# A wave of attention chunks beside an expert layer: three kinds of TensorE work put into one place of the timetable

## The chip, the cores and the metric

The kernel runs on one core of a Trainium2 chip, as one launch. The metric is device time in microseconds: the median of three runs, 939.94 us (939.4 to 940.61). Five engines work side by side and wait for each other through semaphores: TensorE (PE; its weight loads have a row of their own, PEld), VectorE (DVE), ScalarE (ACT), GpSimd (POOL) and SyncE (SP, which issues most DMAs).

## The reference

Three layers follow each other: a linear attention with a decaying state, a bilinear feed-forward layer, and a mixture of eight experts of which each token takes two.

```python
for t in range(S):                     # attention, B=4, H=8, S=768, D=48
    cur = einsum('bhd,bhe->bhde', u[None] * kt, vt)
    y[:, :, t] = einsum('bhd,bhde->bhe', rt, state + cur)
    state = wt[..., None] * state + einsum('bhd,bhe->bhde', kt, vt)
h = (x @ w1) * (x @ w2) @ w3           # x: 3072 x 384, w1, w2: 384 x 1024
x = h @ w_out
logits = x @ w_gate + log1p(exp(x @ w_noise)) * noise   # then the best 2 of 8 experts
out[mask] += weight * (relu(x[mask] @ w1[e]) @ w2[e])
```

## The kernel before

The 3072 tokens are cut into 24 chunks of 128 (j = 0 to 23), six to a batch. A chunk's attention has these parts, each a function of j:

- `pre_scan`, `pre_rec`, `pre_k`, `pre_r` (mostly DVE, `pre_rec` step 0 on ACT) turn decays, keys and queries into scaled keys `kt` and queries `rt`; `pre_u`, `pre_c`, `pre_d` (POOL, DVE, ACT) make the diagonal term, and `pre_d` fills the tile `am` with it.
- `at_A` (A, line 240): key-query products, 8 matmuls on halves of 64 rows of the array (`tile_position` is the row 0 or 64). The trace shows each as two, so 16. `at_ov` then copies them under a mask into `am` (DVE, L245).
- `at_T` (T, L250): 4 transposes of the keys on the full array, copied by ACT into `kn`.
- `at_kv` (kv, L261): state products, 8 matmuls (16 in the trace) on halves of 64 columns of the array; DVE adds and scales them (`sc`, `stmp`, `snew`, L265 to L272), and ACT copies the state into `S`.
- `at_y` (y, L300): outputs, on quarters of 32 columns; 56 matmuls in the trace (32 where a batch begins, since there is no state yet). ACT and DVE split the result into `xh` and `xl`. The last chunk of a batch has no T and no kv.

The feed-forward layer goes in 12 groups of two chunks. A group has 12 places: `mo_ab` eight times (18 matmuls of 256 columns on the full array each: x @ w1 into one bank, x @ w2 into another; ACT copies the first to `ac`, DVE multiplies to `pp`, ACT and `low_p` on DVE split that into `ph` and `pl`) and `mo_x` four times (12 matmuls of 400 columns). All of them are on the full 128x128 array, and they are the filling between the attention parts.

A timetable sets what stands beside what. `at(slot, fn, ...)` puts a call into a list, and `run_todo(slot)` runs the list at the end of the place with that number: slots below 0 lie in the weight folding that comes first (0 to about 65 us), slot 12g+i is place i of group g. So two parts of one slot stand next to each other on every engine, in the order in which they were put in. Before, the attention of chunk j from 4 on begins at slot 6j-12 and takes one slot for each of A, `at_ov`, T, kv and y (`start` and `att_steps`), the preparations lie up to 7 slots earlier (`PRE`), and tables (`ATT`, `PREL`) give the first chunks. DVE runs in written order; the order on the other engines comes from a list scheduler that follows it closely. After the last group (about 450 us) eight experts follow, which the change doesn't touch.

Of the kernel before, what the change touches and what calls it, by code (L numbers as in the profile page):

```python
# [22 lines left out]
NCH = N // P  # L23
CPB = S // P
# [47 lines left out]
def tile_kernel(ctx: ExitStack, tc: tile.TileContext, dt, nat, w3t, wout, w1, w2, e1, e2, cf, ci, out):  # L72
# [17 lines left out]
    def c(n):  # L90
        o, w = CF[n]
        return cft[:, o:o + w]
# [84 lines left out]
    def load_dt(j):  # L177
        DT[j] = att.tile([P, NDT], F32, name="dtc")
        sp.dma_start(out=DT[j], in_=dt[j])

    def load_na(j):
        NA[j] = att.tile([P, NNAT], F32, name="natc")
        sp.dma_start(out=NA[j], in_=nat[j])
# [4 lines left out]
    def pre_scan(j):  # L188
        FG[j] = att.tile([P, 8 * (HC + 1)], F32, name="fg")
        dve.tensor_tensor_scan(out=FG[j], data0=DT[j][:, 8 * P:], data1=d1, initial=0.0,  # L190
                               op0=OP.mult, op1=OP.add)

    def pre_rec(j, step):

        fa = fgv(j)[:, :, 1:]
        if step == 0:
            RC[j] = att.tile([P, 8, HC], F32, name="rc", bufs=1)
            KT[j] = att.tile([P, 4, 2, HC], F32, name="kt")
            act.activation(out=RC[j], in_=fa, func=AF.Ln)
            act.activation(out=RC[j], in_=RC[j], func=AF.Exp, scale=-1.0)  # L200
        else:
            t = KT[j].rearrange("p a s i -> p (a s) i")
            dve.tensor_tensor(out=t, in0=fa, in1=RC[j], op=OP.mult)
            dve.scalar_tensor_tensor(RC[j], t, -2.0, RC[j], op0=OP.add, op1=OP.mult)

    def pre_k(j):
        k = DT[j][:, 4 * P:8 * P].rearrange("p (a s i) -> p a s i", s=2, i=HC)
        dve.tensor_tensor(out=KT[j][:, :, 0], in0=k[:, :, 0], in1=fgv(j)[:, 1::2, :HC], op=OP.mult)
        dve.scalar_tensor_tensor(KT[j][:, :, 1], k[:, :, 1], -1.0, RC[j][:, 0::2], op0=OP.mult, op1=OP.mult)

    def pre_r(j):
        RT[j] = att.tile([P, 4, 2, HC], F32, name="rt")
        r = DT[j][:, :4 * P].rearrange("p (a s i) -> p a s i", s=2, i=HC)
        dve.scalar_tensor_tensor(RT[j][:, :, 0], r[:, :, 0], -1.0, RC[j][:, 1::2], op0=OP.mult, op1=OP.mult)
        dve.tensor_tensor(out=RT[j][:, :, 1], in0=r[:, :, 1], in1=fgv(j)[:, 0::2, :HC], op=OP.mult)

    def pre_u(j):
        t = att.tile([P, DM], F32, name="rku", bufs=1)
        on = dve if 2 <= j < 5 else pool
        on.tensor_tensor(out=t, in0=NA[j][:, :DM], in1=NA[j][:, DM:2 * DM], op=OP.mult)  # L220
        on.tensor_tensor(out=t, in0=t, in1=c("u"), op=OP.mult)
        KS["u", j] = t
# [12 lines left out]
    def at_A(j):  # L235

        for a in range(4):
            for hb in range(2):
                q = slice(HC * hb, HC * hb + D)
                pe.matmul(bST[hb][:, P * a:P * a + P], KT[j][q, a].rearrange("p s i -> p (s i)"),  # L240
                          RT[j][q, a].rearrange("p s i -> p (s i)"), start=True, stop=True,
                          tile_position=(HC * hb, 0))

    def at_ov(j, hb):
        dve.copy_predicated(out=AM[j][:, hb::2], mask=ic("mask")[:, None, :].to_broadcast([P, 4, P]),  # L245
                            data=bST[hb].rearrange("p (h t) -> p h t", h=4))

    def at_T(j):
        for a in range(4):
            pe.transpose(bY[:, P * a:P * a + P], KT[j][:, a].rearrange("p s i -> p (s i)"), ident)  # L250
        KN[j] = att.tile([P, 4, P], F32, name="kn", bufs=1)
        act.copy(out=KN[j].rearrange("p a t -> p (a t)"), in_=bY)
# [4 lines left out]
    def at_kv(j):  # L257
        kv = bK[:, :4 * D].rearrange("p (a e) -> p a e", a=4)
        for a in range(4):
            for hb in range(2):  # L260
                pe.matmul(kv[64 * hb:64 * hb + 64, a], KN[j][:, a, 64 * hb:64 * hb + 64],  # L261
                          vv(j, 2 * a + hb)[:, 16 * hb:16 * hb + D], start=True, stop=True,
                          tile_position=(0, 64 * hb))
        sc = att.tile([P, 4], F32, name="sc")
        dve.tensor_tensor(out=sc, in0=fgv(j)[:, 0::2, HC], in1=fgv(j + 1)[:, 1::2, HC], op=OP.mult)  # L265

        new = att.tile([P, 4, D], F32, name="snew", bufs=2)
        src = kv
        if j % CPB:
            src = att.tile([P, 4, D], F32, name="stmp", bufs=1)  # L270
            dve.tensor_tensor(out=src, in0=kv, in1=KS["s", j], op=OP.add)
        dve.tensor_tensor(out=new, in0=src, in1=sc[:, :, None].to_broadcast([P, 4, D]), op=OP.mult)  # L272
        KS["s", j + 1] = new
        for hb in range(2):
            q = slice(64 * hb, 64 * hb + D)
            act.copy(out=St[(j + 1) % 2][q, :, D * hb:D * hb + D], in_=new[q])

    def at_y(j):
        first = j % CPB == 0
        yv = bY[:, :3 * P].rearrange("p (k t) -> p k t", k=3)  # L280
        qs = []
        for q in range(4):
            lst = []
            for kb in range(3):
                a, b = PIECES[kb][q]
                if b is None:
                    hs, so = ((a, 32 * (a % 2)),), 64 * (a % 2)
                else:
                    hs, so = ((a, 32), (b, 0)), 32
                ms = [(vv(j, h)[:, o:o + 32], AM[j][:, h, :]) for h, o in hs]  # L290
                if not first:
                    ms.append((St[j % 2][:, a // 2, so:so + 32], RT[j][:, a // 2].rearrange("p s i -> p (s i)")))
                for i, (lt, rh) in enumerate(ms):
                    lst.append((yv[32 * q:32 * q + 32, kb], lt, rh, i == 0, i == len(ms) - 1, (0, 32 * q)))
            qs.append(lst)
        for i in range(max(map(len, qs))):
            for q in range(4):
                if i < len(qs[q]):
                    o, lt, rh, st, en, tp = qs[q][i]
                    pe.matmul(o, lt, rh, start=st, stop=en, tile_position=tp)  # L300
        g, s = divmod(j, 2)
        if s == 0:
            XH[g] = xp.tile([P, 3, 2 * P], F32R, name="xh")
            XL[g] = xp.tile([P, 3, 2 * P], F32R, name="xl")
        h, l = XH[g][:, :, s * P:s * P + P], XL[g][:, :, s * P:s * P + P]
        act.copy(out=h, in_=yv)
        dve.tensor_tensor(out=l, in0=yv, in1=f(h), op=OP.subtract)

    def att_steps(j):
        last = j % CPB == CPB - 1  # L310

        def s0():
            at_A(j)

        def s1():
            at_ov(j, 0)
            at_ov(j, 1)

        def s2():
            if not last:  # L320
                at_T(j)

        def s3():
            if not last:
                at_kv(j)

        def s4():
            at_y(j)
            if j + 2 < NCH:
                load_na(j + 2)  # L330

        return [s0, s1, s2, s3, s4]

    def pre_steps(j):
        def p2():
            pre_k(j)
            pre_r(j)
            if j + 2 < NCH:
                load_dt(j + 2)

        return [lambda: pre_scan(j), lambda: pre_rec(j, 0), lambda: pre_rec(j, 1), p2, lambda: pre_u(j),
                lambda: pre_c(j), lambda: pre_d(j)]


    woh, wol = [w.rearrange("p (j d) -> p j d", d=XW) for w in (WBh, WBl)]
# [56 lines left out]
    def at(slot, fn, *a):  # L402
        todo.setdefault(slot, []).append((fn, a))
# [2 lines left out]
        for fn, a in todo.pop(k, []):  # L406
            fn(*a)

    def start(j):
        return 6 * (j - 2)  # L410

    PRE = (-7, -7, -4, -3, -2, -2, -1)
    PREL = {0: (-21, -20, -18, -17, -19, -16, -14), 1: (-15, -14, -13, -12, -14, -12, -11),
            2: (-10, -9, 1, 1, -4, 2, 2), 3: (1, 1, 4, 5, 3, 5, 6)}
    ATT = {0: (-14, -13, -14, -13, -12), 1: (-10, -9, -10, -9, -8), 2: (4, 5, 5, 6, 7), 3: (8, 9, 9, 10, 11)}
    WLD = {(0, 0): -16, (0, 1): -14, (1, 0): -8, (1, 1): -6, (0, 2): -4, (1, 2): -2, (0, 3): 1, (1, 3): 3}
    WCV = {(0, 0): -9, (0, 1): -7, (1, 0): -5, (1, 1): -2, (0, 2): 0, (1, 2): 2, (0, 3): 4, (1, 3): 7}
    WSP = (-5, -5, 2, 3)
# [11 lines left out]
            at(slot, cv_w, *k, i)  # L430
    for k, slot in WLD.items():
        at(slot, load_w, *k)
    for j in range(NCH):
        for i, fn in enumerate(att_steps(j)):
            at(ATT[j][i] if j < 4 else start(j) + i, fn)
    for j in range(NCH):
        lo = ATT[j - 2][4] if 2 <= j < 6 else start(j - 2) + 4
        for i, fn in enumerate(pre_steps(j)):
            at(PREL[j][i] if j < 4 else max(lo, start(j) + PRE[i]), fn)
    for slot in WCV.values():  # L440
        if slot >= -5:
            at(slot + 1, flush, 1)
# [590 lines left out]
```

## Time and profile before

| | us |
|---|---|
| median of three runs | 939.94 |
| the profiled execution | 938.21 |
| its span | 936.4 |
| PE busy | 910.5 (97%) |
| PEld busy | 841.4 (90%) |
| DVE busy | 447.3 (48%) |
| ACT busy | 421.9 (45%) |
| POOL busy | 330.3 (35%) |

The profiled execution's span runs from the first instruction to the last; 1.8 us lie around it. A busy PE is not PE at its peak, since the ends of matmuls are modelled and matmuls overlap. What tells how fast PE gets on is the distance from the start of one matmul to the start of the next. In a timeline each row has the start, the time from the first start to the last end of what is merged in the row, the engine, the line, output and input, the shape of the array that is used, the shape of the data and the count.

### The profile page before, as it was taken

How to read it: one execution, taken by the hardware profiler on the slowest of the kernel's cores; microseconds unless marked ns; L12 is line 12 of the kernel's file. 1: busy time of each engine (PE TensorE's matmuls, PEld its weight loads, DVE VectorE, ACT ScalarE, POOL GpSimd, SP SyncE). 2: the span in 40 equal slices, each digit the busy share in tenths (PEclk: the TensorE clock that was granted, in tenths of full speed). 3: DMA queues.
4: the chain of work that ended last, by engine and by line, in shares of the span. 5: the costliest groups of instructions: out<-in, count | busy, mean ns of one | idle time of the engine just before them, and what ended most of it. 6: DMA issues, size and time to landing. Idle time of an engine off the chain costs nothing.

```text
span 936.4 us, 17811 instructions
## 1 busy us (share of the span) xinstructions
PE 910.5 (97%) x7235; PEld 841.4 (90%) x7235; DVE 447.3 (48%) x1126; ACT 421.9 (45%) x875; POOL 330.3 (35%) x267
## 2 busy tenths in 40 slices
PE   8998899999999999999999999999999999999994
PEld 6787799999999999999989989899998989989894
DVE  5889676656665756657364452331313123131320
ACT  7776546446446445454352343433323343332420
POOL 1100110232222131130506626655556565555422
PEclk9999999999999999999999999999999999999997
DMA  9945876445232242220231645344172533614112
GB/s 357 385 157 176 196 139 212 152 139 185 80 117 89 80 125 81 94 77 19 77 128 37 143 135 162 60 133 101 32 172 65 158 64 89 145 28 105 18 20 36
DMA packets 49179, 111.64 MB, mean 119 GB/s; under 512 B 17600, under 2 KB 32192, under 8 KB 49088
## 3 DMA queue, kind: packets, MB, share of 16 engines
q1 hardware_dynamic: 33472, 85.98, 28.6%
q0 software_dynamic: 12160, 19.72, 12.0%
q10 hardware_dynamic: 3456, 4.72, 1.4%
q8 instruction: 58, 0.95, 0.4%
q14 instruction: 33, 0.27, 0.1%
HBM read 88.12 MB, written 22.27 MB: 118 GB/s over the span
## 4 chain that ended last, share of the span: by engine, by line
PE 90%; DVE 4%; ACT 2%; DMA 1%; issue 1%; POOL 0%; POOLq 0%; SPq 0%; ACTq 0%; DVEq 0%
PE pb L170 27%; PE pb L171 26%; PE pb L172 26%; PE pb L300 3%; PE pb L240 2%; PE pb L740 2%; PE pb L778 1%; PE pb L261 1%; PE pb L250 1%; DVE cvz L154 1%; ACT top L145 1%; PE pb L371 0%; DMA raw<-w 0%; ACT w3h L156 0%; DMA rawf<-wout 0%
## 5 line engine op out<-in xcount | busy, mean ns | idle before, releaser
L170 PE MATMUL pb<-XTh,WAh 128*128 128x512 f32 (+1 forms) x384 | 133.3, 348 | 0.0
L171 PE MATMUL pb<-XTl,WAh 128*128 128x512 f32 (+1 forms) x384 | 131.8, 343 | 0.0
L170 PE MATMUL pb<-WBh,HH 128*128 128x384 f32 x384 | 130.9, 341 | 0.0
L172 PE MATMUL pb<-XTh,WAl 128*128 128x512 f32 (+1 forms) x384 | 130.9, 343 | 0.0
L171 PE MATMUL pb<-WBl,HH 128*128 128x384 f32 x384 | 129.6, 337 | 0.0
L172 PE MATMUL pb<-WBh,HH 128*128 128x384 f32 x384 | 129.5, 337 | 0.0
L756 DVE SCALAR_TENSOR_TENSOR HH<-pb,HH 128x256 fp32r<-128x256 f32 (+1 forms) x128 | 71.3, 558 | 116.0 <-ACT HH L755 116.0
L783 POOL DMA_INDIRECT out<-ye,ti x56 | 87.2, 1557 | 107.5 <-ACT ye L773 94.3
L755 ACT ACTIVATE HH<-pb 128x256 fp32r<-128x256 f32 (+1 forms) x128 | 62.8, 491 | 125.0 <-PE pb L172 123.9
L643 POOL DMA_INDIRECT slots<-g_sc,g_si x48 | 52.2, 1088 | 137.0 <-DVE g_si L642 90.8
L220 POOL TENSOR_TENSOR rku<-natc 128x384 f32<-128x384 f32 x21 | 22.1, 1052 | 212.0 <-DMA natc<-nat 139.4
L773 ACT ACTIVATE ye<-pb,ti 128x384 f32<-128x384 f32 x48 | 27.9, 582 | 145.5 <-PE pb L172 129.7
L124 DVE TENSOR_TENSOR XTl<-pb,XTh 128x512 fp32r<-128x512 f32 (+1 forms) x48 | 25.2, 569 | 130.4 <-ACT XTh L123 130.4
L170 PE MATMUL pb<-xh,WBh 128*128 128x256 f32 x288 | 84.0, 291 | 1.7 <-ACT WAh L156 1.4
L170 PE MATMUL pb<-xh,WAh 128*128 128x256 f32 x288 | 82.7, 287 | 1.6 <-DVE W1l L124 1.2
L172 PE MATMUL pb<-xh,WBl 128*128 128x256 f32 x288 | 81.4, 283 | 1.3 <-DVE WBl L161 1.3
L171 PE MATMUL pb<-xl,WBh 128*128 128x256 f32 x288 | 82.2, 285 | 0.0
L172 PE MATMUL pb<-xh,WAl 128*128 128x256 f32 x288 | 81.2, 282 | 0.4 <-DVE WAl L161 0.4
L171 PE MATMUL pb<-xl,WAh 128*128 128x256 f32 x288 | 81.1, 282 | 0.0
L170 PEld LDWEIGHTS pb<-XTh,WAh 128*128 128x128 f32 x384 | 72.2, 188 | 9.6 <-DVE HH L756 1.5
L171 PEld LDWEIGHTS pb<-XTl,WAh 128*128 128x128 f32 x384 | 72.2, 188 | 8.0
L172 PEld LDWEIGHTS pb<-XTh,WAl 128*128 128x128 f32 x384 | 71.8, 188 | 8.2
(174 smaller groups left out, 2185.4 us busy)
## 6 DMA issues: line engine op xcount, KB each, us to landing
dtc<-dt SPq DMA_DIRECT2D x24, 772.0 KB, 4.4
natc<-nat SPq DMA_DIRECT2D x24, 640.0 KB, 5.9
raw<-e SPq DMA_DIRECT2D x18, 768.0 KB, 6.8
raww<-e SPq DMA_DIRECT2D x14, 768.0 KB, 4.4
rawf<-w3t SPq DMA_DIRECT2D x16, 512.0 KB, 7.7
raw<-w SPq DMA_DIRECT2D x8, 768.0 KB, 5.3
x_rows<-xo ACTq DMA_DIRECT2D x24, 192.0 KB, 1.9
out<-zeros SPq DMA_DIRECT2D x4, 1152.0 KB
```

Source lines behind the costliest of these rows:

```text
L124: (on or dve).tensor_tensor(out=l, in0=src, in1=f(h), op=OP.subtract)
L170: pe.matmul(o, wh, xh, start=start, stop=False)
L171: pe.matmul(o, wh, xl, start=False, stop=False)
L172: pe.matmul(o, wl, xh, start=False, stop=stop)
L220: on.tensor_tensor(out=t, in0=NA[j][:, :DM], in1=NA[j][:, DM:2 * DM], op=OP.mult)
L240: pe.matmul(bST[hb][:, P * a:P * a + P], KT[j][q, a].rearrange("p s i -> p (s i)"), RT[j][q, a].rearrange("p s i -> p (s i)"), start=True, ...
L300: pe.matmul(o, lt, rh, start=st, stop=en, tile_position=tp)
L643: ins = pool.indirect_dma_start(out=table, out_offset=bass.IndirectOffsetOnAxis(ap=si[:, i, k:k + 1], axis=0), in_=SC[:, i, k, :], in_offs ...
L755: act.activation(out=Hh[hf][:, ff], in_=bank[:, :n], func=AF.Relu)
L756: dve.scalar_tensor_tensor(Hl[hf][:, ff], bank[:, :n], 0.0, f(Hh[hf][:, ff]), op0=OP.max, op1=OP.subtract)
L773: act.activation(out=y[:n], in_=bank[:n], func=AF.Copy, scale=wt)
L783: ins = pool.indirect_dma_start(out=out, out_offset=bass.IndirectOffsetOnAxis(ap=ti(e, j)[:, 0:1], axis=0), in_=y[:n], in_offset=None, com ...
```

## The change

The slots of the attention parts are moved, and nothing else. For chunk j from 6 on: kv and y of chunk j and A of chunk j+1 share slot 6j-8 (in this order), `at_ov` of j+1 is in the slot behind, and T of chunk j is in slot 6j-11, three before its kv. The scan stands in slot 6j-20, `pre_rec` step 0 in 6j-19, step 1 in 6j-18, `pre_k` in 6j-17, `pre_r` and `pre_c` in 6j-16, `pre_u` in 6j-17, `pre_d` in 6j-15. A table `WHEN` has chunks 0 to 5. Within a slot the order is now that of `STEPS`. No instruction is added or taken away.

```diff
--- before.py
+++ after.py
@@ -306,40 +306,30 @@
         act.copy(out=h, in_=yv)
         dve.tensor_tensor(out=l, in0=yv, in1=f(h), op=OP.subtract)
 
-    def att_steps(j):
-        last = j % CPB == CPB - 1
-
-        def s0():
-            at_A(j)
-
-        def s1():
-            at_ov(j, 0)
-            at_ov(j, 1)
-
-        def s2():
-            if not last:
-                at_T(j)
-
-        def s3():
-            if not last:
-                at_kv(j)
-
-        def s4():
-            at_y(j)
-            if j + 2 < NCH:
-                load_na(j + 2)
-
-        return [s0, s1, s2, s3, s4]
-
-    def pre_steps(j):
-        def p2():
-            pre_k(j)
-            pre_r(j)
-            if j + 2 < NCH:
-                load_dt(j + 2)
-
-        return [lambda: pre_scan(j), lambda: pre_rec(j, 0), lambda: pre_rec(j, 1), p2, lambda: pre_u(j),
-                lambda: pre_c(j), lambda: pre_d(j)]
+    def do_y(j):
+        at_y(j)
+        if j + 2 < NCH:
+            load_na(j + 2)
+
+    def do_kv(j):
+        if j % CPB < CPB - 1:
+            at_kv(j)
+
+    def do_T(j):
+        if j % CPB < CPB - 1:
+            at_T(j)
+
+    def do_ov(j):
+        at_ov(j, 0)
+        at_ov(j, 1)
+
+    def do_r(j):
+        pre_r(j)
+        if j + 2 < NCH:
+            load_dt(j + 2)
+
+    STEPS = (do_kv, do_y, at_A, do_ov, do_T, pre_scan, lambda j: pre_rec(j, 1), pre_k, do_r, lambda j: pre_rec(j, 0),
+             pre_u, pre_c, pre_d)
 
 
     woh, wol = [w.rearrange("p (j d) -> p j d", d=XW) for w in (WBh, WBl)]
@@ -406,13 +396,13 @@
         for fn, a in todo.pop(k, []):
             fn(*a)
 
-    def start(j):
-        return 6 * (j - 2)
-
-    PRE = (-7, -7, -4, -3, -2, -2, -1)
-    PREL = {0: (-21, -20, -18, -17, -19, -16, -14), 1: (-15, -14, -13, -12, -14, -12, -11),
-            2: (-10, -9, 1, 1, -4, 2, 2), 3: (1, 1, 4, 5, 3, 5, 6)}
-    ATT = {0: (-14, -13, -14, -13, -12), 1: (-10, -9, -10, -9, -8), 2: (4, 5, 5, 6, 7), 3: (8, 9, 9, 10, 11)}
+    WHEN = {0: (-13, -12, -14, -13, -14, -21, -18, -17, -17, -20, -19, -16, -14),
+            1: (-9, -8, -10, -9, -10, -15, -13, -12, -12, -14, -14, -12, -11),
+            2: (6, 7, 4, 5, 5, -10, 1, 1, 1, -9, -4, 2, 2),
+            3: (11, 11, 8, 9, 9, 1, 4, 5, 5, 1, 3, 5, 6),
+            4: (16, 16, 11, 12, 13, 7, 8, 9, 9, 7, 10, 10, 11),
+            5: (22, 22, 16, 17, 19, 11, 13, 14, 14, 12, 13, 14, 15)}
+    LATE = (6, 6, 0, 1, 3, -6, -4, -3, -2, -5, -3, -2, -1)
     WLD = {(0, 0): -16, (0, 1): -14, (1, 0): -8, (1, 1): -6, (0, 2): -4, (1, 2): -2, (0, 3): 1, (1, 3): 3}
     WCV = {(0, 0): -9, (0, 1): -7, (1, 0): -5, (1, 1): -2, (0, 2): 0, (1, 2): 2, (0, 3): 4, (1, 3): 7}
     WSP = (-5, -5, 2, 3)
@@ -430,13 +420,9 @@
             at(slot, cv_w, *k, i)
     for k, slot in WLD.items():
         at(slot, load_w, *k)
-    for j in range(NCH):
-        for i, fn in enumerate(att_steps(j)):
-            at(ATT[j][i] if j < 4 else start(j) + i, fn)
-    for j in range(NCH):
-        lo = ATT[j - 2][4] if 2 <= j < 6 else start(j - 2) + 4
-        for i, fn in enumerate(pre_steps(j)):
-            at(PREL[j][i] if j < 4 else max(lo, start(j) + PRE[i]), fn)
+    for i, fn in enumerate(STEPS):
+        for j in range(NCH):
+            at(WHEN[j][i] if j in WHEN else 6 * j - 14 + LATE[i], fn, j)
     for slot in WCV.values():
         if slot >= -5:
             at(slot + 1, flush, 1)
```

PE, chunk 10 and the key-query products of chunk 11, before: kv (L261) stands alone between full-array matmuls; 17 of these come before y (L300), and 30 more before A (L240).

```order
L170 MATMUL pb_67<-xh,WBh 128x256
L261 MATMUL pb_73<-natc,kn 64x48 x8
L171 MATMUL pb_67<-xl,WBh 128x256
...
L172 MATMUL pb_67<-xh,WBl 128x256
L300 MATMUL pb_70<-am,natc 32x128 x4
...
L300 MATMUL pb_70<-rt,S_102 32x128 x4
L170 MATMUL pb_68<-W0h,ph 128x400
...
L172 MATMUL pb_66<-xh,WAl 128x256
L240 MATMUL pb_71<-rt,kt 128x128
...
L240 MATMUL pb_72<-rt,kt 128x128
L170 MATMUL pb_67<-xh,WBh 128x256
```

The same in the changed kernel:

```order
L172 MATMUL pb_67<-xh,WBl 128x256
L261 MATMUL pb_73<-natc,kn 64x48 x8
L300 MATMUL pb_70<-am,natc 32x128 x4
...
L300 MATMUL pb_70<-rt,S_102 32x128 x4
L240 MATMUL pb_71<-rt,kt 128x128
...
L240 MATMUL pb_72<-rt,kt 128x128
L170 MATMUL pb_68<-W0h,ph 128x400
```

kv, y and A now follow each other with no full-array matmul between them. Counted over the program, kv and y of a chunk touch in 16 chunks (4, 6 to 10, 12 to 16, 18 to 22), and y of a chunk touches A of the next in 19 (these, and 5, 11 and 17, which have no kv). Chunk 3 keeps them apart, and its kv is cut in two, with 8 full-array matmuls between.

DVE in slot 1, before: `kt` and `rt` of chunk 2 (L203 to L215), then the scan of chunk 3 (`fg`, L190).

```order
L512 TENSOR_TENSOR pp<-ac,pb_67 128x512
L203 TENSOR_TENSOR kt<-fg,rc 128x512
L204 SCALAR_TENSOR_TENSOR rc<-kt,rc 128x512
L208 TENSOR_TENSOR kt<-dtc,fg 128x4x64
L209 SCALAR_TENSOR_TENSOR kt<-dtc,rc 128x4x64
L214 SCALAR_TENSOR_TENSOR rt<-dtc,rc 128x4x64
L215 TENSOR_TENSOR rt<-dtc,fg 128x4x64
L190 SCALAR_TENSOR_TENSOR fg<-dtc,d_80 128x520
```

In the changed kernel (its L498 is L512 of before):

```order
L498 TENSOR_TENSOR pp<-ac,pb_67 128x512
L190 SCALAR_TENSOR_TENSOR fg<-dtc,d_80 128x520
L203 TENSOR_TENSOR kt<-fg,rc 128x512
L204 SCALAR_TENSOR_TENSOR rc<-kt,rc 128x512
L208 TENSOR_TENSOR kt<-dtc,fg 128x4x64
L209 SCALAR_TENSOR_TENSOR kt<-dtc,rc 128x4x64
L214 SCALAR_TENSOR_TENSOR rt<-dtc,rc 128x4x64
L215 TENSOR_TENSOR rt<-dtc,fg 128x4x64
```

The scan of chunk 3 now stands ahead of the keys and queries of chunk 2, which A of chunk 2 waits for.

DVE in slots 10 and 11, before: the state of chunk 3 (`sc`, `stmp`, `snew`), then the diagonal of chunk 4 (`rku`, `cc`), then `pl`.

```order
L512 TENSOR_TENSOR pp<-ac,pb_67 128x512
L265 TENSOR_TENSOR sc<-fg 128x4
L271 TENSOR_TENSOR stmp<-pb_73,snew 128x192
L272 TENSOR_TENSOR snew<-stmp,sc 128x192
L220 TENSOR_TENSOR rku<-natc 128x384
L221 TENSOR_TENSOR rku<-rku,cft 128x384
L227 TENSOR_REDUCE cc<-rku 128x8
L522 TENSOR_TENSOR pl<-pp,ph 128x512
```

In the changed kernel (L498 is L512 of before, L508 is L522):

```order
L498 TENSOR_TENSOR pp<-ac,pb_67 128x512
L220 TENSOR_TENSOR rku<-natc 128x384
L221 TENSOR_TENSOR rku<-rku,cft 128x384
L227 TENSOR_REDUCE cc<-rku 128x8
L508 TENSOR_TENSOR pl<-pp,ph 128x512
L265 TENSOR_TENSOR sc<-fg 128x4
L271 TENSOR_TENSOR stmp<-pb_73,snew 128x192
L272 TENSOR_TENSOR snew<-stmp,sc 128x192
```

The state's three instructions now stand behind `pl`, which `mo_x` waits for.

## Rows read from the trace of the kernel before

**Rows 1.** The page: busy time of each engine, share of the span, instructions.

```profile
PE 910.5 (97%) x7235; PEld 841.4 (90%) x7235; DVE 447.3 (48%) x1126; ACT 421.9 (45%) x875; POOL 330.3 (35%) x267
```

**Rows 2.** The page: the chain that ended last, by engine.

```profile
PE 90%; DVE 4%; ACT 2%; DMA 1%; issue 1%; POOL 0%; POOLq 0%; SPq 0%; ACTq 0%; DVEq 0%
```

**Rows 3.** Busy us of each engine (instructions) in two stretches, PE clock, DMA.

```profile
100.00:120.00 20.00, 17.25 (x181) 15.50 (x182) 14.07 (x29) 9.61 (x23) 2.78 (x2) 1.00 0.97 135
120.00:140.00 20.00, 20.00 (x230) 19.06 (x232) 13.37 (x25) 7.58 (x18) 2.35 (x2) 1.00 0.64 157
```

**Rows 4.** Timeline of PE around kv of chunk 10.

```profile
222.38 0.28 PE L172 MATMUL pb<-xh,WAl 128*128 128x256 f32 x1
222.50 0.28 PE L170 MATMUL pb<-xh,WBh 128*128 128x256 f32 x1
222.71 0.67 PE L261 MATMUL pb<-natc,kn 128*64 128x48 f32 x16
223.31 0.39 PE L171 MATMUL pb<-xl,WBh 128*128 128x256 f32 x1
223.54 0.28 PE L172 MATMUL pb<-xh,WBl 128*128 128x256 f32 x1
```

**Rows 5.** Timeline of PE around y of chunk 10.

```profile
225.34 0.28 PE L172 MATMUL pb<-xh,WBl 128*128 128x256 f32 x1
225.54 0.43 PE L300 MATMUL pb<-am,natc 128*32 128x128 f32 x8
...
226.88 0.40 PE L300 MATMUL pb<-rt,S 128*32 128x128 f32 x8
227.21 0.45 PE L170 MATMUL pb<-W0h,ph 128*128 128x400 f32 x1
227.50 0.34 PE L171 MATMUL pb<-W0l,ph 128*128 128x400 f32 x1
227.68 0.34 PE L172 MATMUL pb<-W0h,pl 128*128 128x400 f32 x1
```

**Rows 6.** Timeline of PE around A of chunk 11.

```profile
231.52 0.28 PE L172 MATMUL pb<-xh,WAl 128*128 128x256 f32 x1
231.73 1.16 PE L240 MATMUL pb<-rt,kt 48*128 48x128 f32 x16
232.82 0.38 PE L170 MATMUL pb<-xh,WBh 128*128 128x256 f32 x1
233.04 0.28 PE L171 MATMUL pb<-xl,WBh 128*128 128x256 f32 x1
```

**Rows 7.** PE, groups by line, 120 to 430 us: count | busy us, mean ns | idle.

```profile
L300 PE MATMUL pb<-rt,S 128*32 128x128 f32 x360 | 21.8, 273 | 0.0
L240 PE MATMUL pb<-rt,kt 48*128 48x128 f32 x288 | 20.9, 285 | 0.0
L261 PE MATMUL pb<-natc,kn 128*64 128x48 f32 x256 | 10.8, 226 | 0.0
```

**Rows 8.** Timeline of DVE, scan of chunk 3, and state of chunk 3.

```profile
79.09 1.24 DVE L190 TENSOR_TENSOR_SCAN fg<-dtc,d 128x520 f32<-128x520 f32 x1
...
108.82 0.16 DVE L265 TENSOR_TENSOR sc<-fg 128x4 f32<-128x4 f32 x1
...
109.56 0.55 DVE L220 TENSOR_TENSOR rku<-natc 128x384 f32<-128x384 f32 x1
```

**Rows 9.** Timeline of PE, A of chunk 2, and a wait for `pl`.

```profile
79.40 1.16 PE L240 MATMUL pb<-rt,kt 48*128 48x128 f32 x16
...
111.95 0.45 PE L172 MATMUL pb<-W1h,pl 128*128 128x400 f32 x1 [1.33 <-DVE pl L522]
```

**Rows 10.** Timeline of ACT after kv and y of chunk 10.

```profile
224.22 0.71 ACT L276 COPY S<-snew 48x192 f32<-48x192 f32 x2 [0.93 <-DVE snew L272]
...
227.35 0.48 ACT L306 CAST xh<-pb 128x384 fp32r<-128x384 f32 x1 [0.28 <-PE pb L300]
```

**Rows 11.** Timeline of DVE after y of chunk 10.

```profile
227.86 0.56 DVE L307 TENSOR_TENSOR xl<-pb,xh 128x384 fp32r<-128x384 f32 x1 [1.45 <-ACT xh L306]
```

## The prediction

> **What bounds the kernel now.** The page's first part comes first: PE is busy 97% of the span, DVE and ACT under half [rows 1]. The reader is to see that a gain has to come out of PE's own time. The chain of waits agrees: 90% of it is PE [rows 2]. Then the stretches of 20 us, since an average hides stages: from 120 us on PE is busy 20.00 of 20.00 us, at a granted clock of 1.00 (2.4 GHz), in each of the 15 stretches up to 420 us, while between 100 and 120 us it has 17.25 [rows 3]. So in the groups from 1 on no other engine ever ends a wait of PE; there only the distance from one matmul's start to the next one's counts. Before that, PE waits now and then, and a move can cost or give there. After 450 us the program is the same.
>
> The last view is PE's timeline around one chunk, read by starts. Among full-array matmuls a 256-column one starts 0.12 us after the one before (222.38 to 222.50) [rows 4], after a 400-column one it is 0.18 us (227.50 to 227.68) [rows 5]. Where the shape of the array changes, the distance is longer, in three places of each visit:
> - Going in. Before kv 222.50 to 222.71 is 0.21 us, 0.09 over the usual 0.12 [rows 4]; before y 0.20, so 0.08 over [rows 5]; before A 0.21, so 0.09 over [rows 6].
> - Coming out. A merged row ends with its last matmul's end, so the last start is the row's start plus its length less one matmul (226, 273 and 285 ns) [rows 7]. kv: 222.71 + 0.67 - 0.23 = 223.15; eight pairs make seven steps, 0.44 / 7 = 0.06 each; the full matmul starts at 223.31, 0.16 later, 0.10 over a step [rows 4]. y: 226.88 + 0.40 - 0.27 = 227.01; 14 rounds of four make 13 steps from 225.54, 0.11 each; the next one comes 0.20 later, 0.09 over [rows 5]. A: 231.73 + 1.16 - 0.29 = 232.60, steps of 0.125, then 0.22, so 0.09 over [rows 6].
> - The first full matmul after a visit, whose weights could not be loaded ahead. It holds the next one up to 0.23 us instead of 0.12 behind kv [rows 4], 0.29 instead of 0.18 behind y [rows 5], 0.22 instead of 0.12 behind A [rows 6]: 0.11, 0.11 and 0.10 over.
>
> So a visit pays about 0.09 going in and 0.09 + 0.11 coming out, whatever its shape.
>
> **The change, part by part.** Nothing is computed less: the order of PE before and after has the same matmuls.
>
> *Joins.* Where two visits stand side by side, the first one's way out (0.09 + 0.11) and the second one's way in (0.09), 0.29 together, are replaced by one change from one tiling to another. No row shows such a change: in the kernel before every visit to kv, y or A in the groups has full-array matmuls on both sides. From below it may cost nothing (then 0.29 is saved); from above as much as the way by the full array, 0.29 (nothing is saved), and no reason excludes that it is dearer still. I take 0.09, because going in and coming out cost 0.08 to 0.10 in all six rows, with three different tilings on one side. That looks like one price for any change of shape, and the 0.11 on top belongs to the full array's weights, which a join does not load. Each join then saves 0.29 - 0.09 = 0.20 us. The order has 16 joins of kv with y and 19 of y with A, 35 in all: 35 x 0.20 = 7.0 us. All of it lies on the bound engine in a stretch where nothing else ends its waits, so all of it should come off the time.
>
> The Trainium skill says in "TensorEngine Tiling (Array Packing)", section Tiling Modes, Key Properties, that a change of the tiling mode, though not of the tile alone, drains TensorE. That rule speaks against the larger gain: by it a join still pays a drain and the sum is 7.0 us, without it 35 x 0.29 = 10.2 us. The trace agrees with it for changes to and from the full array, and can't say it of a change between two tilings.
>
> *T three places ahead of kv.* The transposes run on the full array, so their place changes no join. It gives ACT's `kn` copy two more places before kv needs it. It saves nothing where kv doesn't wait today, and from 120 us on it does not [rows 3]. Cost 0.
>
> *The first chunks.* Three things change there, of opposite sign. (a) In slot 1 the scan of chunk 3, 1.24 us, now goes ahead of the keys and queries of chunk 2, and A of chunk 2, which started at 79.40, waits for them [rows 8, 9]. DVE's work up to what is needed next is the same, so the waits for DVE that follow shrink: between 0 and 1.2 us, I take 0.4 lost. (b) In slots 10 and 11 the state of chunk 3 (`sc`, `stmp`, `snew`: 108.82 to 109.56, so 0.74 us) moves behind `pl`, and PE stood 1.33 us for that `pl` at 111.95 [rows 8, 9]: 0 to 0.74 us gained, I take 0.7, since nothing else stands between. (c) For chunks 0 and 1 the same three instructions go ahead of the masked copy that y waits for, up to 0.74 us each [rows 8], and kv of chunk 3 is cut in two, one more visit of 0.29 us: 0 to 1.8 us lost, I take 0.3, since most of it falls beside waits that exist already. Sum 0.7 - 0.4 - 0.3 = 0; its ends are 3.0 us lost (0 - 1.2 - 1.8) and 0.7 gained.
>
> *The work that must still hide.* Now the state, the output and the next scan come to DVE and ACT in one place. SP's issues keep their order but for one (the keys of chunk 4 go ahead of the table's first filling), POOL's writes of slots are split by `rku` two and two, and nobody on PE waits for those in this stretch. DVE runs the scan ahead of `pl`, which has three places (over 6 us) before `mo_x` uses it, so 1.24 us more is covered. The output is what is late next, and it is the slower rival below.
>
> Sum: the profiled execution takes 938.21 us, 7.0 less is 931.2. The median of the runs is 1.73 us above that execution; 939.94 - 7.0 = **932.9 us**. What a measurement of this kernel can tell from no change is about 0.2%, 1.9 us.
>
> **The rivals.**
> 1. *A join is free.* For it: tilings share no weights that would have to wait, and the 0.11 us belongs to the full array. Against: coming out of a tiling costs 0.09 before any reload shows. Then 35 x 0.29 = 10.2 us, about 929.7; if the first narrow weights hide as well, somewhat less.
> 2. *A join costs as much as the way by the full array.* For it: no row shows a join, and a narrow tile's first weights are no more loaded ahead than full ones. Against: the full array's weights are no longer loaded in between, so their 0.11 us can't be paid there. Then 939.9, within 0.2%.
> 3. *Half is lost.* The first chunks come out at their bad end of 3.0 us, which leaves 4.0 (935.9), or a few joins wait for an operand besides. For it: PE has only 17.25 of 20 us between 100 and 120 us [rows 3], so DVE and ACT set the pace there. Against: the waits that exist hide part of what is added. About 936.3.
> 4. *Slower: the output of every second chunk comes late.* xh now stands behind the two state copies on ACT, which wait for `snew` on DVE, which waits for kv; before, kv was a place earlier. The output of chunks 5, 7, ... 21 (nine) is the operand of the next group's first matmul. From the start of the last full matmul ahead, by rows: kv ends after 0.21 + 0.67 = 0.9 us; the state takes DVE 0.74 [rows 8] and ACT 0.71 [rows 10], at 0.1 for each handing over (xh stood 0.07 behind y's end, xl 0.03 behind xh) [rows 10, 11], so 2.6; y ends at about 2.5; xh 0.48 and xl 0.56 with their handing over bring it to 3.8. PE meanwhile needs 0.21 + 0.44 + 0.16 + 1.43 + 0.20 + 0.88 + 0.21 = 3.5 us for kv, y and A, 0.3 for the first full matmul and 11 x 0.18 = 2.0 for the others of `mo_x`: 5.8. The cover is 2.0 us. The gain is eaten when the chain is 2.0 + 7.0 / 9 = 2.8 us later than that; 3.5 us of lateness would cost 9 x 1.5 = 13.5, so about 946. For it: `xl` stood 1.45 us for xh and the state copies 0.93 us for `snew` in the row [rows 10, 11]. Against: A itself is the cover, 1.3 us that was not there before.
>
> **How the numbers follow.** Forecast 0.64 (931 to 935 by itself: 6.0 to 8.0 from the joins, 1 us for the first chunks), free join 0.12, half lost 0.12, no saving 0.06, slower 0.06. Faster by over 0.2% are the forecast, the free join and half lost: 0.88; same 0.06; slower 0.06. The range goes from 928, below the free join, to 937.5, above half lost, and leaves out no saving and slower, 0.12.
>
> **What would show it.** In the profile after, PE's timeline of chunk 10 has kv, y and A in one block, 0.15 to 0.17 us from the last kv start to the first y start and 0.20 to 0.22 from the last y start to the first A start; a free join would show 0.06 and 0.11, a dear one over 0.3. The block is 0.40 us shorter than the three visits before. The stretch from y of chunk 6 to y of chunk 22, all PE, with 30 joins in it, is shorter by about 30 x 0.20 = 6.0 us. PE stays at 20.00 of 20. Wrong would be: idle PE before a group's first matmul (rival 4); a wait before A of chunk 2 of over 1.2 us; or a gain that comes from after 450 us.

## The result, and the profile after

The changed kernel takes 945.79 us (median of five runs, 944.57 to 947.23), the kernel before 939.94. The ratio is 1.0061, with a 95% interval of 1.0043 to 1.0079. So it is slower by about 6 us, where 932.9 was forecast. The profiled execution took 945.79 us, with a span of 944.0 (936.4 before).

Stages first, each from the first y matmul of one chunk to that of another on PE:

| stretch | before, us | after, us | difference |
|---|---|---|---|
| start of the span to y of chunk 0 | 46.6 | 48.0 | +1.4 |
| y of chunk 0 to y of chunk 5 | 92.69 | 92.44 | -0.25 |
| **y of chunk 5 to y of chunk 6** | 17.37 | 28.81 | **+11.44** |
| **y of chunk 6 to y of chunk 22** | 273.63 | 268.38 | **-5.25** |
| y of chunk 22 to the first matmul of the experts | 50.70 | 50.97 | +0.27 |
| from there to PE's last matmul | 442.85 | 442.89 | +0.04 |
| from there to the end of the span | 12.54 | 12.50 | -0.04 |

The saving came, and one stretch of some 28 us lost twice as much. The page's two lines after, busy time and the chain by engine, against [rows 1, 2], show little of that:

```profile
PE 909.2 (96%) x7235; PEld 843.2 (89%) x7235; DVE 461.1 (49%) x1126; ACT 422.3 (45%) x875; POOL 331.0 (35%) x267
```

```profile
PE 87%; DVE 4%; ACT 4%; DMA 2%; issue 1%; POOL 1%; POOLq 0%; SPq 0%; ACTq 0%; DVEq 0%
```

PE is busy 1.3 us less in a span that is 7.6 us longer, and some of the chain has gone from PE to ACT and DMA. An average over 944 us can't say where. The windows after can (busy us of PE, PEld, DVE, ACT and POOL, then PE's clock and DMA), against [rows 3]:

```profile
100.00:120.00 20.00, 17.26 (x176) 14.97 (x176) 15.50 (x28) 9.37 (x22) 2.85 (x2) 1.00 0.44 152
120.00:140.00 20.00, 20.00 (x215) 19.49 (x215) 12.78 (x27) 8.74 (x21) 0.00 (x0) 1.00 1.04 90
140.00:160.00 20.00, 10.15 (x112) 9.06 (x111) 5.74 (x9) 5.40 (x14) 3.98 (x4) 0.74 0.66 214
```

Between 140 and 160 us PE has 10.15 of 20 us, where it had all of them before, and its clock there is 0.74. Between 100 and 120 us it has what it had, and from 160 to 440 us all of every 20 us. In the stretch ahead of the loss the DMA engines are full (1.04) and yet move only 90 GB/s, and POOL does nothing.

**The joins.** PE's timeline after, around chunk 10 (start, length of the row, engine, line, tiles, shapes, count), against [rows 4 to 6]:

```profile
235.89 0.28 PE L172 MATMUL pb<-xh,WBl 128*128 128x256 f32 x1
236.11 0.67 PE L261 MATMUL pb<-natc,kn 128*64 128x48 f32 x16
236.71 0.43 PE L300 MATMUL pb<-am,natc 128*32 128x128 f32 x8
...
238.04 0.40 PE L300 MATMUL pb<-rt,S 128*32 128x128 f32 x8
238.38 1.16 PE L240 MATMUL pb<-rt,kt 48*128 48x128 f32 x16
239.47 0.45 PE L170 MATMUL pb<-W0h,ph 128*128 128x400 f32 x1
239.75 0.35 PE L171 MATMUL pb<-W0l,ph 128*128 128x400 f32 x1
```

Read by starts: the last kv start is 236.11 + 0.67 - 0.23 = 236.55, y comes 0.16 later; the last y start is 238.04 + 0.40 - 0.27 = 238.17, A comes 0.21 later. Over all chunks the means are 0.152 us (16 joins) and 0.202 (19). The three visits with what they cost going in and out take 3.56 us (235.89 to 239.75, less two usual steps of 0.12 and 0.18), against 3.95 before, added up in the same way, 0.39 less.

**The lost stretch.** PE's timeline after, where the group that takes chunks 4 and 5 begins; the brackets show the idle time ahead and who ended it:

```profile
145.31 0.34 PE L172 MATMUL pb<-W1h,pl 128*128 128x400 f32 x1
155.49 0.58 PE L170 MATMUL pb<-xh,WAh 128*128 128x256 f32 x1 [9.84 <-ACT xh L306]
...
158.60 0.41 PE L170 MATMUL pb<-xh,WAh 128*128 128x256 f32 x1
158.81 0.34 PE L171 MATMUL pb<-xl,WAh 128*128 128x256 f32 x1
```

One wait of 9.84 us for `xh` of chunk 5. From 155.49 to 158.81 13 matmuls start, 0.21 us and more apart instead of 0.12: 3.32 us for 1.56. These 1.76 and the 9.84 make 11.6, about the 11.4 of the table. But `xh` is only the last of a chain. The waits after, 118 to 165 us (engine and what it waited for: us in all, times, longest):

```profile
POOL rku L220 <- DMA natc<-nat: 33.1, 2, 31.8
ACT am L233 <- DVE cc L227: 16.7, 2, 16.2
DVE cc L227 <- POOL rku L221: 14.2, 1, 14.2
...
PE pb L170 <- ACT xh L306: 9.8, 1, 9.8
```

Followed back from PE: PE waits for ACT (9.8 us), ACT for DVE (16.2), DVE for POOL (14.2), POOL for a load (31.8). The load `natc` is that of chunk 6. SP's queue after, where it is issued (start and length of the issue, target and source):

```profile
123.45 0.33 SPq L179 DMA_DIRECT2D dtc<-dt  x1
123.83 7.93 SPq L640 DMA_DIRECT2D slots<-cit  x3
131.80 1.86 SPq L643 DMA_DIRECT2D x_rows<-zeros  x1
133.75 2.30 SPq L183 DMA_DIRECT2D natc<-nat  x1
```

The same four before:

```profile
107.08 9.63 SPq L654 DMA_DIRECT2D slots<-cit  x3
116.76 1.11 SPq L657 DMA_DIRECT2D x_rows<-zeros  x1
123.08 0.36 SPq L179 DMA_DIRECT2D dtc<-dt  x1
125.13 0.35 SPq L183 DMA_DIRECT2D natc<-nat  x1
```

Before, SP issued the filling of the expert table (`fill_table`) at 107 us, and then stood waiting with the keys of chunk 7 (`dtc`), whose buffer comes free when DVE has made `rt` of chunk 5. Now the keys stand first: they wait 14.2 us, until 123.45, and the filling, which waits for nothing, goes out behind them and directly ahead of `natc`. That is then issued 8.6 us later than before (133.75 and 125.13). What the filling puts into the queue is in the view of the DMA engines after, 129 to 134 us (its last two lines give KB and the us from issue to landing):

```profile
DMA packets 4635, 0.07 MB, mean 14 GB/s; under 512 B 4635, under 2 KB 4635, under 8 KB 4635
...
x_rows<-zeros SPq DMA_DIRECT2D x1, 1344.0 KB, 14.6
natc<-nat SPq DMA_DIRECT2D x1, 640.0 KB, 15.1
```

In these 5 us the engines carry nothing but packets of some 15 bytes (0.07 MB in 4635), 14 GB/s in all. The filling also ends with 1344 KB of zeros for `x_rows`, and these stand between the small packets and `natc`. Over 134 to 144 us the engines move 112 GB/s, over 144 to 149 410 GB/s. So `natc` stands behind small packets and behind zeros, and no run tells the share of each.

POOL's first instruction on it, after and before:

```profile
148.95 0.99 POOL L220 TENSOR_TENSOR rku<-natc 128x384 f32<-128x384 f32 x1 [31.78 <-DMA natc<-nat]
```

```profile
134.62 1.01 POOL L220 TENSOR_TENSOR rku<-natc 128x384 f32<-128x384 f32 x1 [19.21 <-DMA natc<-nat]
```

From its issue `natc` takes 15.2 us after and 9.5 before. So the operand is 14.3 us later: 8.6 in the issue and 5.7 in the queue. DVE's timeline after shows what stands behind it, then ACT's after, and then DVE's before:

```profile
151.04 0.55 DVE L227 TENSOR_REDUCE cc<-rku 128x8 f32<-128x384 f32 x1 [14.20 <-POOL rku L221]
153.41 0.69 DVE L498 TENSOR_TENSOR pp<-ac,pb 128x512 f32<-128x512 f32 x1 [1.81 <-ACT ac L495]
155.47 0.56 DVE L307 TENSOR_TENSOR xl<-pb,xh 128x384 fp32r<-128x384 f32 x1 [1.37 <-ACT xh L306]
```

```profile
151.63 1.28 ACT L233 ACTIVATE am<-cft,cc 128x128 f32<-128x128 f32 x4 [16.18 <-DVE cc L227]
...
154.97 0.47 ACT L306 CAST xh<-pb 128x384 fp32r<-128x384 f32 x1
```

```profile
141.63 0.56 DVE L307 TENSOR_TENSOR xl<-pb,xh 128x384 fp32r<-128x384 f32 x1 [1.24 <-ACT xh L306]
142.11 0.54 DVE L227 TENSOR_REDUCE cc<-rku 128x8 f32<-128x384 f32 x1
```

Before, `cc` of chunk 6 stood behind `xl` of chunk 5; now it stands two places sooner, ahead of it and of a `pp`. So it holds up DVE, and `am` behind it holds up ACT ahead of `xh`, which the next group's first matmul needs.

### The profile page after: what moved, and what is told of

Same layout as the page of the kernel before. It is cut to its first block, busy times and chain, and to the rows that moved or that the text cites. A ratio compares the mean times of both kernels' runs of the same rounds, so it can differ in the third digit from the quotient of the medians.

```text
span 944.0 us, 17811 instructions
## 1 busy us (share of the span) xinstructions
PE 909.2 (96%) x7235; PEld 843.2 (89%) x7235; DVE 461.1 (49%) x1126; ACT 422.3 (45%) x875; POOL 331.0 (35%) x267
## 3 DMA queue, kind: packets, MB, share of 16 engines
q0 software_dynamic: 12160, 19.72, 11.6%
## 4 chain that ended last, share of the span: by engine, by line
PE 87%; DVE 4%; ACT 4%; DMA 2%; issue 1%; POOL 1%; POOLq 0%; SPq 0%; ACTq 0%; DVEq 0%
PE pb L170 26%; PE pb L171 25%; PE pb L172 25%; PE pb L300 3%; PE pb L240 2%; PE pb L726 2%; DMA natc<-nat 2%; PE pb L764 1%; PE pb L261 1%; ACT am L233 1%; PE pb L250 1%; ACT top L145 1%; DVE cvz L154 1%; DMA raw<-w 0%; DVE am L245 0%
## 5 line engine op out<-in xcount | busy, mean ns | idle before, releaser
L233 ACT ACTIVATE am<-cft,cc 128x128 f32<-128x128 f32 x192 | 61.3, 393 | 51.3 <-DVE cc L227 51.2
L170 PE MATMUL pb<-xh,WBh 128*128 128x256 f32 x288 | 81.4, 283 | 1.0 <-DVE pp L498 1.0
```

The source lines that it names most:

```text
L170: pe.matmul(o, wh, xh, start=start, stop=False)
L233: act.activation(out=AM[j][:, h], in_=ident, func=AF.Copy, scale=KS["c", j][:, h:h + 1])
```

## The experiments

Two moves meet in that chain: the filling behind the keys (theory S, SP's queue) and `cc` ahead of `xl` (theory C, DVE's order). The first runs tell them apart; the runs are called e1 to e8. Everywhere the ratio is that to the kernel before on the same chip; on the chip of e1, e2, e3 and e7 the kernel before took 945.77 us, on the others 939.62 and 939.5, so ratios are compared and not times, and a time that was expected is read as a share of 939.94.

**e1. The filling first, in the changed kernel.** It is put ahead of `load_dt` of chunk 7 in its slot; `cc` stays early.

```diff
+    at(SPG + 2, lambda: fill_table())
     for i, fn in enumerate(STEPS):
...
-    at(SPG + 2, fill_table)
```

> The changed kernel with one call moved: in slot 14 the first filling of the expert table (L654 of before, SP) stands ahead of the load of keys and queries of chunk 7 again, as in the kernel before. Theory S (SP's queue): in the changed kernel that load, which waits for VectorE's rt of chunk 5 until 123.4 us, held the filling behind it on SP from 107 to 124 us, so the filling's 10 us of issuing fell in front of the load of natc of chunk 6. Then the wait of 9.8 us of PE at 155 us goes, with the stretch at half clock behind it (11.4 us together), the joins stay (0.39 us a chunk): 945.8 - 11.4 = 934.4, 933 to 936. Theory C (the diagonal's sum cc was moved two places sooner on VectorE and that alone makes PE wait): the wait stays, 944 to 947. Theory J (three kinds in one place make the output late): the wait stays too.

Measured: ratio 0.9932 (0.9916 to 0.9949), which is 933.5 of 939.94, as S has it; y of chunk 5 to y of chunk 6 takes 17.0 us. SP's queue, then DVE:

```profile
112.61 9.10 SPq L641 DMA_DIRECT2D slots<-cit  x3
...
126.81 0.36 SPq L179 DMA_DIRECT2D dtc<-dt  x1
129.68 0.35 SPq L183 DMA_DIRECT2D natc<-nat  x1
```

```profile
141.66 0.54 DVE L227 TENSOR_REDUCE cc<-rku 128x8 f32<-128x384 f32 x1
```

`cc`, early as it stands, waits for nothing. The order of two entries of one slot decided between slower by 0.6% and faster by 0.7%.

**e2. The filling late, in the kernel before.** The other side: the old timetable, with the filling one slot later, hence behind the keys.

```diff
-    at(SPG + 2, fill_table)
+    at(SPG + 3, fill_table)
```

> The kernel before with one call moved: the filling of the expert table stands in slot 15 instead of 14, so behind the load of keys and queries of chunk 7. Nothing is joined. Theory S: natc of chunk 6 is issued about 8 us later than at 125.1 us and lands near 149 instead of 134; cc of chunk 6, due at 142 us here, waits until about 151, so pl behind it is about 3 us late for mo_x: 940 + 3 to 5, 942 to 946. Theory C: cc is at its old place, so nothing waits on PE: 939 to 941.

Measured: 1.0054 (1.0033 to 1.0074), which is 945.0 of 939.94, again as S has it; 21.0 us for the stretch instead of 17.4. DVE, then PE:

```profile
143.15 0.56 DVE L307 TENSOR_TENSOR xl<-pb,xh 128x384 fp32r<-128x384 f32 x1 [1.45 <-ACT xh L306]
150.89 0.55 DVE L227 TENSOR_REDUCE cc<-rku 128x8 f32<-128x384 f32 x1 [7.18 <-POOL rku L221]
151.36 0.68 DVE L522 TENSOR_TENSOR pl<-pp,ph 128x512 fp32r<-128x512 f32 x1
```

```profile
152.09 0.45 PE L172 MATMUL pb<-W1h,pl 128*128 128x400 f32 x1 [1.18 <-DVE pl L522]
...
154.98 0.39 PE L170 MATMUL pb<-xh,WAh 128*128 128x256 f32 x1 [0.35 <-ACT ac L509]
...
159.02 0.67 PE L261 MATMUL pb<-natc,kn 128*64 128x48 f32 x16 [1.51 <-ACT kn L252]
```

`cc` is as late as in the changed kernel (150.89 and 151.04), but `xl` is through by then, so PE waits three times a little instead of once for long. SP's order by itself loses 3.7 us in the stretch, and needs nothing else of the change.

**e3. The diagonal at its old places, in the changed kernel.** For chunks from 6 on `cc` and `am` go back to the old slots, behind `xl`; `rku` goes to 6j-15, one ahead of the old slot that the text below names. The filling stays late.

```diff
-    LATE = (6, 6, 0, 1, 3, -6, -4, -3, -2, -5, -3, -2, -1)
+    LATE = (6, 6, 0, 1, 3, -6, -4, -3, -2, -5, -1, 0, 1)
...
-    for i, fn in enumerate(STEPS):
-        for j in range(NCH):
-            at(WHEN[j][i] if j in WHEN else 6 * j - 14 + LATE[i], fn, j)
+    for i in (0, 1, 2, 12, 3, 4, 5, 6, 7, 8, 9, 10, 11, -1):
+        for j in range(NCH) if 0 <= i < 12 else range(6, NCH) if i > 0 else range(6):
+            at(WHEN[j][i] if j in WHEN else 6 * j - 14 + LATE[i], STEPS[i], j)
```

> The changed kernel with the diagonal (rku, cc, am) at its old slots for chunks from 6 on: 6j-14, 6j-14 and 6j-13 instead of 6j-17, 6j-16 and 6j-15; the filling stays late. Theory S: natc of chunk 6 still lands near 149 us, cc is due some 6 us later than in the changed kernel, and PE waits 2 to 5 us instead of 9.8, with no stretch at half clock: 936 to 940. Theory C: no wait at all, 933 to 935.5. If neither SP's order nor cc's place matters: 944 to 947.

Measured: 0.9922 (0.9907 to 0.9937), 18.0 us for the stretch. DVE, then PE:

```profile
143.52 0.56 DVE L307 TENSOR_TENSOR xl<-pb,xh 128x384 fp32r<-128x384 f32 x1 [1.45 <-ACT xh L306]
...
149.96 0.55 DVE L227 TENSOR_REDUCE cc<-rku 128x8 f32<-128x384 f32 x1 [4.74 <-POOL rku L221]
```

```profile
154.06 0.39 PE L170 MATMUL pb<-xh,WAh 128*128 128x256 f32 x1 [0.70 <-ACT ac L495]
```

`cc` is still as late as 149.96, and yet only 0.70 us of it reaches PE. So the late load alone doesn't make the long wait: it takes the late load and an early `cc`. The same late load behind a late `cc` cost 3.7 us in e2 and costs about 1 us here (18.0 against 17.0 in e1): of the waits of e2, that for `pl` (1.18) and that of kv for `kn` (1.51) are missing. T, which makes `kn`, stands three places ahead here, but no run moves it alone. The 936 to 940 us that S expected were reckoned on a kernel before of 940, so a ratio of 0.996 at the best; 0.9922 is below that.

**e7. The load of chunk 6 alone on ACT's queue, in the changed kernel.** Filling late, `cc` early, and only this `natc` issued by ACT.

```diff
-        sp.dma_start(out=NA[j], in_=nat[j])
+        (act if j == 6 else sp).dma_start(out=NA[j], in_=nat[j])
```

> The changed kernel, but natc of chunk 6 is loaded from ScalarE's queue instead of SP's, so that it does not stand behind the filling there; the filling stays late and its packets run at the same time. If what counts is the place in SP's queue, natc is issued near 127 us instead of 133.75, lands by 139, and PE waits 0 to 3 us: 934 to 938. If what counts is that the DMA engines are full with the filling's small packets, natc lands after 145 us whatever its queue, and PE still waits over 6 us: over 941.

Measured: 0.9936 (0.992 to 0.9952), at the fast end of what the place in SP's queue would give; 17.0 us for the stretch, and PE doesn't wait. The issue on ACT, the filling on SP, and POOL:

```profile
125.83 0.36 ACTq L183 DMA_DIRECT2D natc<-nat  x1
```

```profile
123.31 10.12 SPq L640 DMA_DIRECT2D slots<-cit  x3
```

```profile
133.03 1.01 POOL L220 TENSOR_TENSOR rku<-natc 128x384 f32<-128x384 f32 x1 [16.32 <-DMA natc<-nat]
```

The filling runs as in the changed kernel, and the load, issued in the middle of it, is used 7.2 us later (133.03). So the filling's traffic beside it is not what hurt; standing behind the filling in the same queue is. The Trainium skill says in "DMA: Bandwidth & Descriptors", section Queues, rings and completion order, that each DMA engine takes turns between the queues that have work for it, packet by packet, while within a queue the ring is worked in order. The trace agrees: 7.2 us beside the filling, 15.2 behind it.

**The changed kernel once more.** On another chip, unchanged.

> The changed kernel again, beside the three below on one chip: it fills the fourth field of a two-by-two (filling late or early on SP, cc early or late on VectorE). If both are needed for the long wait, it is the only one of the four that has it: 0.4 to 0.8% over the kernel before, while the other three are 0.5 to 0.9% below it.

Measured: 1.0056 (1.0034 to 1.0079); the waits again:

```profile
PE pb L170 <- ACT xh L306: 7.8, 1, 7.8
```

The same wait in the same place, 2 us shorter.

**e6. Both mends in one.** Filling first and diagonal late.

> The changed kernel with both repairs: the filling ahead of the load of keys and queries of chunk 7, and the diagonal at its old slots from chunk 6 on. If the two are needed together for the wait, the second repair adds little to the first: within 1 us of e1_fill_first, so 0.6 to 0.8% below the kernel before. If the places of the diagonal cost by themselves in every chunk (16 chunks), it is 2 us or more faster than e1_fill_first.

Measured: 0.9941 (0.9921 to 0.9961), 934.3 us beside 939.62; the repetition at the end gave 934.54 beside 939.5.

| filling | `cc` | ratio to before | stretch of chunks 5 to 6, us |
|---|---|---|---|
| late | early (the changed kernel) | 1.0061, 1.0056 | 28.8, 27.0 |
| first | early | 0.9932 | 17.0 |
| late | late | 0.9922 | 18.0 |
| first | late | 0.9941 | 17.0 |

The intervals of the last three overlap; the two mends don't add up, since each of them takes the same wait away.

**e4 and e5. What a join is worth.** In the kernel with the filling first: in e4 kv stands one slot ahead of y again (15 joins go), in e5 A and `at_ov` stand a slot behind y of the chunk before (18 joins go).

```diff
-    LATE = (6, 6, 0, 1, 3, -6, -4, -3, -2, -5, -3, -2, -1)
+    LATE = (5, 6, 0, 1, 3, -6, -4, -3, -2, -5, -3, -2, -1)
```

> e1_fill_first with kv of chunks from 6 on one slot sooner, so that 18 full-array matmuls stand between kv and y again: 15 joins of kv with y are undone, the joins of y with A stay. By the price of a join in the forecast, 0.20 us: 15 x 0.20 = 3.0 us slower than e1_fill_first, some 0.36% below the kernel before instead of 0.68%. If y and A alone made the gain: no difference from e1_fill_first.

```diff
-    LATE = (6, 6, 0, 1, 3, -6, -4, -3, -2, -5, -3, -2, -1)
+    LATE = (6, 6, 1, 2, 3, -6, -4, -3, -2, -5, -3, -2, -1)
```

> e1_fill_first with A and the masked copy of chunks from 6 on one slot later, so that full-array matmuls (12) stand between y and A again: 18 joins of y with A are undone, the 16 of kv with y stay. By the price in the forecast: 18 x 0.20 = 3.6 us slower than e1_fill_first, some 0.3% below the kernel before. If kv and y alone made the gain: no difference.

Measured: kv apart 937.98 us, 0.9983 (0.9968 to 0.9998); A apart 937.0, 0.9968 (0.9954 to 0.9981). The 0.36% below the kernel before that was expected of kv apart lies just outside its interval; A apart has its 0.3%. From y of chunk 6 to y of chunk 22, where nothing but PE counts, the traces of the changed kernel and of e1 have 268.38 us, kv apart 270.94 and A apart 271.41. That is 2.56 us for 14 joins and 3.03 for 16: 0.18 and 0.19 us each. The times say less: e1 ran on another chip, and against e6 on the same one (934.3, which also has the diagonal late) 15 joins cost 3.7 us and 18 cost 2.7.

**e8. The first chunks.** In the kernel with both mends the order within a slot is put back: the scan of chunk 3 behind the keys and queries of chunk 2, the state of chunks 0 and 1 behind the masked copy. e6 ran again beside it.

```diff
-    for i in (0, 1, 2, 12, 3, 4, 5, 6, 7, 8, 9, 10, 11, -1):
+    for i in (12, 3, 0, 1, 2, 4, 6, 7, 8, 5, 9, 10, 11, -1):
```

> e6_both with the order inside a slot put back where it touches the first chunks: the masked copies of chunks 0 and 1 ahead of their state's instructions on VectorE, and the scan of chunk 3 behind the keys and queries of chunk 2. The forecast put these two at 0.4 and 0.3 us lost (of 0 to 1.2 and 0 to 1.8): 0 to 1.5 us faster than e6_again, and A of chunk 2 starts about 1 us earlier against y of chunk 1. If the waits on VectorE and ScalarE behind them take it all back: no difference, within 0.5 us.

> e6_both again, on the same chip as e8_head: 0.5 to 0.8% below the kernel before.

Measured: 934.01 (0.994, 0.9926 to 0.9953) beside 934.54 (0.9944, 0.993 to 0.9957). The trace shows A of chunk 2 following y of chunk 1 after 18.89 us instead of 19.63 and 19.79 in the two traces of e6, and 75.77 us from y of chunk 0 to y of chunk 4 instead of 76.72 and 76.87. So about 1 us is there in the trace, and the times can't tell it from nothing.

## Why the prediction was wrong, step by step

- **The sentence that failed** stands under the work that must still hide: "SP's issues keep their order but for one (the keys of chunk 4 go ahead of the table's first filling) [...] and nobody on PE waits for those in this stretch". It was one exchange, but of the keys of chunk 7, which wait for DVE until 123.45, not of chunk 4. What was queued behind the waiting issue was late by that wait, and then stood in front of what came after: here 10 us of filling in front of `natc` of chunk 6. Nobody on PE waits for the filling; PE waits for what came behind it. The rows to see it were there: SP's queue before has the filling at 107.08 and the keys at 123.08.
- **A second move was not weighed at all.** `pre_c` and `pre_d` go two places sooner. The section on the first chunks and the paragraph on what must hide priced the scan and the state, not `cc`, which now stands on DVE ahead of `xl`. By itself that is free (e1 has it, and gains); it turns a late load into a wait of PE. Late load and late `cc` cost about 1 us in that stretch (e3, 18.0 against 17.0), late load and early `cc` 10 to 12.
- **Joins** were right, and in the place named. 0.152 and 0.202 us between the visits were inside what was to be seen (0.15 to 0.17, 0.20 to 0.22). 30 joins gave 5.25 us where 6.0 was worked out: 0.175 each, 0.18 and 0.19 in the runs that undo them, against 0.20. A change between two tilings costs its 0.09 us, so the joins are not free. The Trainium skill says in "TensorEngine Tiling (Array Packing)", section Tiling Modes, that a change of mode drains TensorE. The 0.09 us agree with that, though no row shows that they are a drain.
- **T three places ahead** cost nothing that a run shows; it was tried only together with the rest. In e2, without it, kv waited 1.51 us for `kn`; in e3, with it, kv doesn't.
- **The first chunks** came out near the 0 that was forecast: 76.46 us from y of chunk 0 to y of chunk 4, 76.56 before. The other eight traces with this order have 76.72 to 76.95, so up to 0.4 us lost. The terms had the right sign. PE's timeline after, against [rows 9]:

```profile
81.53 1.16 PE L240 MATMUL pb<-rt,kt 48*128 48x128 f32 x16
...
113.39 0.45 PE L172 MATMUL pb<-W1h,pl 128*128 128x400 f32 x1 [0.60 <-DVE pl L508]
```

  A of chunk 2 is 19.35 us behind y of chunk 1 instead of 19.02, 0.33 lost for the 0.4 of (a). This trace is the mildest: the other eight have 19.59 to 19.79, so 0.6 to 0.8 lost. The wait for `pl` is 0.60 instead of 1.33, 0.73 gained for the 0.7 of (b). From y of chunk 0 to y of chunk 1 it takes 14.17 instead of 13.75, 0.4 lost for the 0.3 of (c).
- **Rivals.** A free join and a dear join are both out. "Half is lost" is out, since the first chunks lost 0.4 us at most. The slower rival named the right sign, an idle PE ahead of a group's first matmul, and the right instruction, `xh` of an odd chunk, for a reason that did not act. It was to be late behind the state copies, nine times; it was late once, behind `am`, in a chunk that ends a batch and has no state copy. That its price, about 946, lies beside the measured 945.79 is luck: it was nine times 1.5 us, and what came was one wait of 9.84 us with 1.76 behind it. For chunk 10, as for the others from 6 on, PE is never idle after the visits.
- **The sum without the fault.** 932.9 of 939.94 is a ratio of 0.9925. The four kernels that take the long wait away (e1, e3, e6, e7) have 0.9922 to 0.9941, with intervals of about 0.002 to either side. So the terms that were worked out hold to within some 1.5 us together, and the miss is the one queue that was dismissed in half a sentence, with the `cc` that was not weighed.
- **Left over:** the +1.4 us ahead of y of chunk 0. It goes with the clock there and not clearly with the change (below): e2, which has the old order there, starts y of chunk 0 at 48.1 us.

The kernel with both mends is faster than both: 934.3 us beside 939.62, and 934.54 beside 939.5.

## What to carry to other kernels

When code is put in another order, write down for every queue, the DMA-issuing ones too, which two entries changed places, and ask of the one that is now first how long it waits: everything behind it inherits that wait, and comes out in a lump ahead of work that matters. A wait with nothing important behind it is free until something is moved behind it. And an early place for an instruction is only as good as its latest operand: where an engine takes its instructions in order, as DVE and ACT do here, it holds up whatever stands behind it.

## What the runs showed of the hardware that was not expected

- **A load behind a filling.** A `natc` of 640 KB was used 15.2 us after its issue right behind the filling on SP's queue, 9.5 us before the change, 8.9 with the filling first, and 7.2 when ACT issued it during the same filling. Five us of that filling are 4635 packets with 0.07 MB, 1344 KB of zeros come behind them, and the issue of the three DMAs with the small packets held SP's queue for 7.9 to 10.1 us.
- **The clock after an idle PE.** PE stood idle from 145.65 to 155.49 us. Over 140 to 160 us the granted clock is 0.74, and over 155 to 158.8 it is 0.50, the 1.2 GHz level. There 256-column matmuls start 0.21 us apart, then 0.12 again. The wait cost 1.76 us on top of its own length. The repetition, with a wait of 7.81 us, shows the same 0.50 behind it (157 to 160 us).
- **The clock at the start of the program differs from run to run.** From 9 to 12 us it was 1.00 in the run of the kernel before, 0.50 in the changed one, 0.77 in its repetition, which then had 0.50 from 12 to 15; y of chunk 0 started at 46.6, 48.0 and 51.0 us. The change does little there, and what decides it is open: no run was made for it.
